# A parallel S4 + mixture-of-experts kernel: first operands, gates, squares and skip term in another order

## The chip, the cores and the metric

The kernel runs on one core of one Trainium2 chip. Its engines are TensorE (PE, matrix products), VectorE (DVE), ScalarE (ACT), GpSimd (POOL, here used only to issue DMAs that add in memory) and SyncE (SP, which issues the other DMAs). The metric is the device time of one execution in microseconds (us); less is better.

## What is computed

For `u` of 2048 tokens by D = 512 the output is a sum of three terms of the normalized rows:

```python
xn  = layernorm(x)                                   # x = u, over the 512 columns
y   = causal_convolution(xn, K) + xn * Dskip         # S4: K from A, B, C, log_dt; by FFT in the reference
moe = sum over e of gates[:, e] * (silu(xn @ w1[e]) @ w2[e])   # 8 experts, F = 1792
out = x + y + moe
```

The gates are the softmax of `xn @ w_gate` over all 8 experts (the top 8 of 8 are kept). All is float32. The two products of the experts are nearly all of the work on PE.

## The kernel before, in words

**Float32 by halves.** PE multiplies f16. Each operand is split into a high and a low f16 part, and each product is three matmuls (high by high, high by low, low by high). ACT writes a high part, DVE the low one (`hilo`, L432 and L435, for weights; L1181 and L1184 in `activate` for activations). So that the parts don't overflow, each weight matrix of each expert is scaled by a power of two that comes from the sum of its squares: ACT squares the weights as they are loaded (`square`, L429; tiles `pp`), DVE sums the rows (tile `r`, L390), PE sums over the partitions (`tot`, L166), ACT copies the sum out (`st`, L164), and a few short DVE steps make the power of two (`prepass_end`). A split of an expert's weight can't begin before its scale.

**Order of the work.** The loops run over expert e (8), token block tb (4 of 512 tokens) and d (4 groups of weight columns: `DQS`, pairs (0,1), (2,3), (4,5), (6)); each d has four slots s. A place is written (e, tb, d, s). `block()` forms the first product by seven Strassen products (`product`, L1162) in three PSUM tiles `hb`, with partial sums kept by ACT (`scC`, `sE`, `scB`, L1333) and added by DMAs from POOL. `pop(n)` issues second products `y` (L1146 to L1148), `flush` the low parts of the activations. The very first block (0, 0) is `plain()`: 14 products f = 0..13 of 12 matmuls each (L1384), without Strassen sums, in 16 slots of which 14 are used; its list of numbers says how many second products each slot issues, and after each product the activation is issued.

**Lists of side work.** `side`, `early` and `mid` map a place to functions that are issued there; `at(n, f)` counts slots from the start of the program (slot n is tb = n // 16 of expert 0). `slot()` (L1273) issues them, then `work_on(limit)`: the next one or two steps of the queue `work`, made by `plan(e)` for the next expert: squares (`piece_square`), the scale (`piece_end`), the splits of `w1` (`piece_w1`; of each raw weight, and of combined weights `tw` that DVE forms first) and of `w2` (`piece_w2`). Then `bg_run` issues steps of the S4 term, nearly all DVE work, as long as an account (`clock`, in estimated us of PE and DVE time) leaves room: a share of PE's time (`SHARE`). The engines take their instructions in the order of issue; semaphores between them come from the tiles.

**First operands.** Before the first product, `xplain(j)` normalizes 128 tokens (DVE), splits them (ACT high, DVE low) and transposes both parts on PE; `xplain_out(j)` copies the result from PSUM, by ACT for even j and DVE for odd j. `first_square` and `first_split` do the squares and splits of expert 0's `w1`, `first_scales` the scale; `keep_busy` issues matmuls without a use.

**Later operands.** The operands of a Strassen block are sums of quarters of x: `x_stats` (mean and 1/std), `x_sums` (DVE, L237 to L243), `x_high` (ACT, L249), `x_low` (DVE, L255), `x_turn` (PE transposes, L267, then a copy from PSUM by ACT or DVE, L271, L273, L278). The transposes, the gates (`gates_mm`, L339 and L342; `gates_dve`, L348 ff.) and the sums of squares share one PSUM bank, tag `s4`; `take_bank` hands it on. The statistics of the next tokens (`norm_sums`, L196) are DVE work too.

**Out of PSUM, and the skip term.** When the last product of a group of 128 tokens is in, `evacuate` scales it by its gate on ACT (L1124) into a tile `ye`, and a DMA from POOL adds it to `oacc` (L1126). `x + xn * Dskip` comes in by `base` (load, L1101), `base_add` (three DVE steps, L1107 to L1109) and `base_send` (a DMA from POOL), for four tiles of 128 tokens per token block. `ye` and `base` share four buffers, tag `stg`. A block's four `ye` come early in the next token block, at (e, tb + 1, 1, 1).

Of the kernel before, what the change touches and what calls it, by code (L numbers as in the profile page):

```python
# [32 lines left out]
def s4_moe_kernel(  # L33
# [61 lines left out]

    uts = {}

    clock = {"slot": 0, "pe": 0.0, "pe0": 0.0, "dve": 0.0, "dve0": 0.0, "left": 0.0}
    bank = {"out": None, "at": -1}

    def take_bank(out=None):
# [144 lines left out]
    def x_high(g, a):  # L246
        hi = xs_["hi"] = sb.tile([P, 7, TH], F16, tag="ta", name=f"xh{g}_{a}", bufs=1)
        for src, n0, n in xs_["f"]:
            S.copy(hi[:, n0:n0 + n, :].rearrange("p o d -> p (o d)"), src.rearrange("p o d -> p (o d)"))  # L249

    def x_low(g, a):
        hi = xs_["hi"]
# [5 lines left out]
    def x_turn(g, a, q):  # L258

        hi, lo = xs_["hi"], xs_["lo"]  # L260
        xv = xop.rearrange("p o a k t -> p (o a k) t")
        n = min(8, 28 - 8 * q)
        take_bank()
        tp = ps_s.tile([P, 8, P], F16, tag="s4", name=f"tp{g}_{a}_{q}")
        for r in range(n):
            o, b, k = (8 * q + r) // 4, (8 * q + r) // 2 % 2, (8 * q + r) % 2
            T.transpose(tp[:, r, :], (hi, lo)[b][:, o, k * P:(k + 1) * P], ident)  # L267
        if g == 1:
            dst = xv[:, 8 * q:8 * q + n, a * P:(a + 1) * P]
            if q % 2:  # L270
                V.tensor_copy(dst, tp[:, :n, :])  # L271
            else:
                S.copy(dst, tp[:, :n, :])  # L273
            if a and q == 3:
                nc.sync.dma_start(xd[1], xop)
        else:
            xs = sb.tile([P, 8, P], F16, tag="hh", name=f"xs{g}_{a}_{q}", bufs=9)
            S.copy(xs[:, :n, :], tp[:, :n, :])  # L278
            bank["at"] = now()
            nc.sync.dma_start(xd[g].rearrange("p o a k t -> p (o a k) t")[:, 8 * q:8 * q + n, a * P:(a + 1) * P],  # L280
                              xs[:, :n, :])
# [3 lines left out]
    def xplain(j, rs8):  # L285

        xn = sb.tile([P, D], F32, tag="fa", name=f"xn{j}")
        V.tensor_scalar(xn, uts[0][j], mean[:, j:j + 1], rs8[:, j:j + 1], op0=ALU.subtract, op1=ALU.mult)
        hl = sb.tile([P, 2, KT, P], F16, tag=("ta", "tt")[j % 2], name=f"xhl{j}", bufs=1)
        hlf = hl.rearrange("p a k t -> p a (k t)")  # L290
        S.copy(hlf[:, 0, :], xn)
        V.tensor_tensor(hlf[:, 1, :], xn, hlf[:, 0, :], op=ALU.subtract)
        xp[j] = ps_y.tile([P, 2 * KT, P], F16, tag=f"y{j}", name=f"tp{j}")
        for a in range(2):
            for k in range(KT):
                T.transpose(xp[j][:, a * KT + k, :], hl[:, a, k, :], ident)
# [130 lines left out]
    def square(e, w, pr, raw):  # L427
        rf = raw.rearrange("p a c -> p (a c)")
        S.activation(rf, rf, AF.Square, accum_out=rows_of(e, w)[:, pr:pr + 1])  # L429

    def hilo(dst, raw, sc):
        S.activation(dst[:, 0], raw, AF.Copy, scale=sc)  # L432
# [366 lines left out]

    act_later = []  # L800

    def tt_(n):

        return n / 960 + 0.14
# [200 lines left out]
    xplain_out(3)  # L1005
    keep_busy(6, ident)
    sq(5, True)
    sq(6)
    low1()
# [110 lines left out]
    def evacuate(e, i, y):  # L1120
        g = gates_e[e][:, i:i + 1]
        if e < E - 1 or i < NT - TPB:
            t = sb.tile([P, D], F32, tag="stg", name=f"ye{e}_{i}", bufs=4)
            S.activation(t, y, AF.Copy, scale=g)  # L1124
            if e:
                nc.gpsimd.dma_start(oacc[i], t, accum_op=ALU.add)  # L1126
            else:
                nc.sync.dma_start(oacc[i], t)
# [37 lines left out]

    tail = []

    def activate(e, tb, d, src, fh, th, whole=False):


        prs = (0, 1) if whole else DQS[d]
        n = len(prs)
        sc = scales[e]
# [6 lines left out]
        S.activation(ahl[:, 0, :n], fa, AF.Copy, scale=sc[:, 3:4])  # L1181

        def low():
            V.scalar_tensor_tensor(ahl[:, 1, :n], fa, sc[:, 3:4], ahl[:, 0, :n], op0=ALU.mult, op1=ALU.subtract)  # L1184
            clock["dve"] += tt_(n * TH)
            for q, pr in enumerate(prs):
# [24 lines left out]
        lows.append((first_split(2), True, False))  # L1211
    early, mid = {}, {}

    def at(n, f, where=side):
# [26 lines left out]
    for tb in range(NB):  # L1241
        for j in range(TPB):
            i = tb * TPB + j
            eb = (1, tb) if tb < NB - 1 else (2, 0)
            put((*eb, 1 + j // 2, j % 2), lambda i=i: base(i))
            put((*eb, 1 + j // 2, 2 + j % 2), lambda i=i: base_add(i))
            put((*eb, 1 + (j + 1) // 2, (3, 1)[j % 2]), lambda i=i: base_send(i))
        put((0, tb, 2, 0), lambda tb=tb: gates_mm(tb))
        put((0, tb, 2, 1), lambda tb=tb: gates_dve(tb))
# [6 lines left out]
    for n, (g, a) in enumerate(halves):  # L1256
# [13 lines left out]
    def slot(e, tb, d, s, pops):  # L1270
# [8 lines left out]
        for f in side.get((e, tb, d, s), ()):  # L1279
            f()  # L1280
        work_lows()
        work_on(2 if tb == NB - 1 or tb == 0 or e == 0 else 1)
        if (e, tb, d, s) >= (0, 2, 3, 1):
            if (e, tb, d, s) == (0, 2, 3, 1):
                clock["pe"] = clock["pe0"] = clock["dve"] = clock["dve0"] = 0.0
            bg_run()
        clock["slot"] += 1

# [19 lines left out]
    def block(e, tb, d):  # L1308
# [22 lines left out]
        def keep(tag, src):  # L1331
            t = sb.tile([P, 2, TH], F32, tag="sE" if tag == "sE" else "sCB", name=f"{tag}{e}_{tb}_{d}", bufs=1 if tag == "sE" else 3)
            S.copy(t[:, :n], src[:, :n])  # L1333
            return t
        begin(0)
        prod(A, 0, 0, True)
        S.copy(B[:, :n], A[:, :n])  # L1337
        if later:
            later.pop(0)()
        slot(e, tb, d, 0, pops[0])  # L1340
# [32 lines left out]
    def plain():  # L1373

        for f in range(NF):
# [90 lines left out]
```

## Time and profile before

| | us |
|---|---|
| median of 3 runs | 2415.65 |
| lowest, highest | 2413.35, 2416.8 |
| the profiled execution's own time | 2415.3 |
| its span, first to last instruction | 2413.5 |
| PE busy | 2354.6 |
| DVE busy | 1955.1 |
| ACT busy | 1426.2 |
| POOL busy | 339.2 |

A row of a timeline gives the start and the duration of an instruction (or of several alike, x12), its engine, line, operation, and out<-in; a bracket gives the idle time of the engine ahead of it and what ended it. In a list of waits a row gives total, number and longest. The granted clock is a share of TensorE's full speed; its mean over the span was 0.993.

### The profile page before, as it was taken

The page shows a single profiled execution, that of the slowest core. Times are in us where ns is not written, and L with a number is a line of the kernel's source. Part 1 is how long each engine was busy: PE and PEld are TensorE (multiplying, and loading weights), DVE is VectorE, ACT ScalarE, POOL GpSimd, SP SyncE. Part 2 cuts the span into 40 slices and gives each one's busy share as a digit, 9 for nine tenths or more (in the row PEclk, how much of TensorE's full clock was granted, in tenths as well). Part 3 has the DMA queues.
Part 4 walks back from the last instruction along what each step waited for, and adds up shares of the span by engine and source line. Part 5 has one row for each costly group of instructions (what it writes and reads, how often), then busy time and mean ns, then how long its engine had stood idle before and what let it go on. Part 6 is the DMA issues. An engine that isn't in the chain of part 4 may idle for free.

```text
span 2413.5 us, 44927 instructions
## 1 busy us (share of the span) xinstructions
PE 2354.6 (98%) x17663; PEld 1564.7 (65%) x17663; DVE 1955.1 (81%) x3836; ACT 1426.2 (59%) x2435; POOL 339.2 (14%) x394
## 2 busy tenths in 40 slices
PE   7789999999999999999999999999999999999999
PEld 4466666666666666666666666666666666666665
DVE  7663588689985999998889799999898799999611
ACT  6477575555646657565675566665575655754443
POOL 0000001211121110111110111111111101111112
PEclk9899999999999999999999999999999999999999
DMA  6466366574664645565465554655555644633356
GB/s 223 144 164 192 74 173 150 132 176 86 175 144 112 133 98 163 108 135 117 106 162 118 120 132 99 160 116 123 122 115 140 143 110 105 165 65 72 76 115 149
DMA packets 264644, 314.41 MB, mean 130 GB/s; under 512 B 124464, under 2 KB 158768, under 8 KB 264112
## 3 DMA queue, kind: packets, MB, share of 16 engines
q1 hardware_dynamic: 208560, 217.93, 29.6%
q0 software_dynamic: 55872, 93.61, 24.5%
q8 instruction: 138, 2.26, 0.4%
q14 instruction: 74, 0.61, 0.1%
HBM read 201.09 MB, written 60.82 MB: 109 GB/s over the span
## 4 chain that ended last, share of the span: by engine, by line
PE 82%; issue 7%; ACT 4%; DVE 3%; DMA 1%; POOL 1%; SPq 0%; DVEq 0%; POOLq 0%; ACTq 0%
PE hb L1162 36%; PE y L1146 14%; PE y L1148 14%; PE y L1147 14%; PE kgen L690 1%; ACT w1s L432 1%; PE yp L791 1%; PE kf L742 1%; PE uf L731 1%; PE hb L1384 1%; PE tp L267 1%; DVE w1s L435 1%; ACT fa L1179 0%; DMA oacc<-ye 0%; ACT ahl L1181 0%
## 5 line engine op out<-in xcount | busy, mean ns | idle before, releaser
L1162 PE MATMUL hb<-xop,w1s 128*128 128x256 f16 x9114 | 1074.9, 273 | 9.1 <-ACT scC L1333 6.8
L1162 PEld LDWEIGHTS <-w1s 128*128 128x128 f16 x9114 | 889.9, 98 | 186.9 <-issue 11.7
L1146 PE MATMUL y<-w2s,ahl 128*128 128x512 f16 x1792 | 680.6, 380 | 10.2 <-ACT ye L1124 10.2
L1148 PE MATMUL y<-w2s,ahl 128*128 128x512 f16 x1792 | 680.9, 380 | 0.0
L1147 PE MATMUL y<-w2s,ahl 128*128 128x512 f16 x1792 | 680.8, 380 | 0.0
L1148 PEld LDWEIGHTS <-ahl 128*128 128x128 f16 x1792 | 175.4, 98 | 212.1 <-issue 0.8
L1306 POOL DMA_DIRECT2D scC<-sE x124 | 111.6, 900 | 1363.6 <-ACT sE L1333 880.2
L1147 PEld LDWEIGHTS <-ahl 128*128 128x128 f16 x1792 | 175.4, 98 | 177.4 <-issue 12.3
L1146 PEld LDWEIGHTS <-ahl 128*128 128x128 f16 x1792 | 175.4, 98 | 165.2 <-issue 0.8
L774 DVE TENSOR_TENSOR s<-s,tm 128x720 f32<-128x720 f32 (+14 forms) x480 | 269.0, 560 | 16.6
L773 DVE TENSOR_TENSOR tm<-v,k 128x720 f32<-128x720 f32 (+14 forms) x480 | 267.7, 558 | 10.9
L1184 DVE SCALAR_TENSOR_TENSOR ahl<-fa,sc,ahl 128x512 f16<-128x512 f32 (+1 forms) x262 | 178.8, 683 | 90.1 <-ACT ahl L1181 90.0
L1179 ACT ACTIVATE fa<-hb,sc 128x512 f32<-128x512 f32 (+1 forms) x252 | 160.0, 635 | 149.7 <-PE hb L1162 141.1
L1344 ACT COPY hb<-hb 128x512 f32<-128x512 f32 x124 | 64.1, 517 | 261.6 <-PE hb L1162 261.6
L1181 ACT ACTIVATE ahl<-fa,sc 128x512 f16<-128x512 f32 (+1 forms) x262 | 175.9, 671 | 8.6
L1306 POOL DMA_DIRECT2D scB<-sE x124 | 107.2, 864 | 421.5 <-ACT scB L1333 291.1
L1184 DVE SCALAR_TENSOR_TENSOR ahl<-scB,sc,ahl 128x512 f16<-128x512 f32 x124 | 84.4, 681 | 100.0 <-ACT ahl L1181 98.6
L1337 ACT COPY hb<-hb 128x512 f32<-128x512 f32 x124 | 64.4, 519 | 167.1 <-PE hb L1162 165.6
L678 DVE TENSOR_TENSOR tb<-ta,tt 128x64 f32<-128x64 f32 (+2 forms) x192 | 132.2, 689 | 6.6
L676 DVE TENSOR_TENSOR ta<-tb,zr 128x64 f32<-128x64 f32 (+2 forms) x192 | 131.3, 684 | 3.4
L1126 POOL DMA_DIRECT2D oacc<-ye x108 | 96.1, 1308 | 259.9 <-ACT ye L1124 257.2
L677 DVE TENSOR_TENSOR tt<-tb,zi 128x64 f32<-128x64 f32 (+2 forms) x192 | 130.5, 680 | 0.0
(256 smaller groups left out, 2399.1 us busy)
## 6 DMA issues: line engine op xcount, KB each, us to landing
xop<-xd SPq DMA_DIRECT2D x210, 256.0 KB, 3.7
pp<-in_w_dram SPq DMA_DIRECT2D x98, 512.0 KB, 4.4
raw<-in_w_dram SPq DMA_DIRECT2D x56, 512.0 KB, 5.1
oacc<-ye POOLq DMA_DIRECT2D x108, 256.0 KB, 6.5
scC<-sE POOLq DMA_DIRECT2D x93, 256.0 KB, 4.2
scB<-sE POOLq DMA_DIRECT2D x93, 256.0 KB, 4.2
raw<-in_w_dram SPq DMA_DIRECT2D x52, 256.0 KB, 4.0
raw<-in_w_dram SPq DMA_DIRECT2D x104, 128.0 KB, 4.1
```

Source lines behind the costliest of these rows:

```text
L676: V.tensor_tensor(ta, tin, zrv, op=ALU.mult)
L678: V.tensor_tensor(tout, ta, tt, op=ALU.add)
L773: V.tensor_tensor(tm, v3f[:, :, 0:n], kb, op=ALU.mult)
L774: V.tensor_tensor(s3[:, :, m:], s3[:, :, m:], tm, op=ALU.add)
L1146: T.matmul(y, lhs[0], w2s[pr][:, 0, fh, :], start=(c == 0), stop=False)
L1147: T.matmul(y, lhs[0], w2s[pr][:, 1, fh, :], start=False, stop=False)
L1148: T.matmul(y, lhs[1], w2s[pr][:, 0, fh, :], start=False, stop=(c == NF - 1))
L1162: T.matmul(dst[:, q, :], w1s[pr][:, a, wo, k * P:(k + 1) * P], xop[:, xo, b, k, :], start=(first_mm and q == 0 and n == 0), stop=(n == 5), ...
L1179: S.activation(fa, src[:, :n], AF.Silu, scale=w1_unscale(e, d if whole else prs[0]))
L1181: S.activation(ahl[:, 0, :n], fa, AF.Copy, scale=sc[:, 3:4])
L1184: V.scalar_tensor_tensor(ahl[:, 1, :n], fa, sc[:, 3:4], ahl[:, 0, :n], op0=ALU.mult, op1=ALU.subtract)
L1306: nc.gpsimd.dma_start(dst, src, accum_op=ALU.add)
```

## The change

1. **First operands.** `xplain` is cut in two: the second half (`xplain_turn`: low part and transposes) is issued later. All four token groups come before the third square of `w1`; only j = 2 is copied out by DVE.
2. **First block.** The activation of f = 0 is issued behind product f = 1; the splits of `w1`, the squares and the scale of `w2` move by a slot or so; `norm_sums(1)` moves ahead of the sum of the `w2` squares (slot 5); the list of second products has fewer early and more late; `gates_split` goes to slot 12 and the gates of the first block to slots 16 and 17, which lie in (0, 1).
3. **Squares.** `clock["act"]` counts ACT's estimated time. Outside (0, 0) and the last token block of an expert, `work_on` gets a step only if the account has over 1.0 us of room (2 steps if 2.2 in expert 0). Before it was 2 steps in token blocks 0 and 3 and in expert 0, otherwise 1.
4. **Sums of squares** (`piece_end`) keep out of the slot before one in which `x_turn` comes (`turns`).
5. **Skip term.** Token blocks go to (1,1), (1,2), (2,1), (2,2) instead of (1,0), (1,1), (1,2), (2,0); both loads of a pair are issued in slot 0 of d = 1 (and d = 2), the sums in slots 1 and 2, both sends in slot 3.
6. `SHARE` is 1.0 instead of 0.96.

```diff
...
     def xplain(j, rs8):
-        hlf = hl.rearrange("p a k t -> p a (k t)")
-        S.copy(hlf[:, 0, :], xn)
-        V.tensor_tensor(hlf[:, 1, :], xn, hlf[:, 0, :], op=ALU.subtract)
+        S.copy(hl[:, 0].rearrange("p k t -> p (k t)"), xn)
+        xp[j] = (xn, hl)
+
+    def xplain_turn(j):
+
+        xn, hl = xp[j]
+        V.tensor_tensor(hl[:, 1].rearrange("p k t -> p (k t)"), xn, hl[:, 0].rearrange("p k t -> p (k t)"), op=ALU.subtract)
...
-        if j % 2:
+        if j == 2:
             V.tensor_copy(dst, xp[j])
...
         def later():
-            return now() > st["at"] + 1 and bank_free()
+            return now() > st["at"] + 1 and bank_free() and now() + 1 not in turns
...
+    def at_(n):
+
+        return n / 1050 + 0.17
...
     sq(0)
     sq(1)
     xplain(0, rs8_0)
+    xplain(1, rs8_0)
+    xplain_turn(0)
     V.tensor_reduce(row2[:, 0:1], rows_of(0, 0)[:, 0:2], axis=AX.X, op=ALU.add)
-    keep_busy(8, ident)
+    sq(2)
     stA = pow2_total(row2[:, 0:1], 1, "a")
     take_bank()
-    xplain(1, rs8_0)
+    xplain_turn(1)
+    keep_busy(8, ident)
+    xplain(2, rs8_0)
...
-    sq(2)
     xplain_out(0)
+    xplain_turn(2)
     low0 = first_split(0)
+    xplain(3, rs8_0)
     keep_busy(8, ident)
-    xplain(2, rs8_0)
+    xplain_out(1)
+    xplain_turn(3)
+    xplain_out(2)
     low0()
+    xplain_out(3)
+    keep_busy(8, ident)
     sq(3)
-    xplain_out(1)
-    keep_busy(8, ident)
-    xplain(3, rs8_0)
     sq(4)
-    xplain_out(2)
     low1 = first_split(1)
-    xplain_out(3)
-    keep_busy(6, ident)
...
-    SHARE = 0.96
+    SHARE = 1.0
...
+    def act_room():
+
+        clock["actleft"] = min(clock["actleft"], 2.0) + clock["pe"] - clock["pe1"] - clock["act"] + clock["act0"]
+        clock["pe1"], clock["act0"] = clock["pe"], clock["act"]
+        return clock["actleft"]
...
     for n in range(7):
-        at(n // 2, lambda n=n: first_square(1, n, second[n], n % 2 == 1))
-    at(0, first_scales, mid)
-    at(0, third)
+        at((n + 1) // 2, lambda n=n: first_square(1, n, second[n], n % 2 == 1))
+    at(1, first_scales, mid)
+    at(1, third)
     for n in range(4):
-        at(2 * n + 1, lambda n=n: plain_split(3 + n))
-    at(4, lambda: next(end_w2))
-    at(5, lambda: next(end_w2), mid)
-    at(6, lambda: fin(end_w2))
-    at(6, lambda: done.add("w2 scale"))
-    at(6, gates_split)
-    at(4, lambda: norm_sums(1))
+        at((2, 4, 5, 7)[n], lambda n=n: plain_split(3 + n))
+    at(5, lambda: norm_sums(1))
+    at(5, lambda: next(end_w2))
+    at(6, lambda: next(end_w2), mid)
+    at(7, lambda: fin(end_w2))
+    at(7, lambda: done.add("w2 scale"))
     at(7, lambda: x_stats(1))
+    at(12, gates_split)
+    at(16, lambda: gates_mm(0))
+    at(17, lambda: gates_dve(0))
...
-            eb = (1, tb) if tb < NB - 1 else (2, 0)
-            put((*eb, 1 + j // 2, j % 2), lambda i=i: base(i))
-            put((*eb, 1 + j // 2, 2 + j % 2), lambda i=i: base_add(i))
-            put((*eb, 1 + (j + 1) // 2, (3, 1)[j % 2]), lambda i=i: base_send(i))
+            eb = (1 + tb // 2, 1 + tb % 2)
+            put((*eb, 1 + j // 2, 0), lambda i=i: base(i))
+            put((*eb, 1 + j // 2, 1 + j % 2), lambda i=i: base_add(i))
+            put((*eb, 1 + j // 2, 3), lambda i=i: base_send(i))
...
         for q in range(4):
             at(s0 + 3 + q // 2, lambda g=g, a=a, q=q: x_turn(g, a, q), mid if q % 2 else early)
+            turns.add(s0 + 3 + q // 2 - 2)
...
-        work_on(2 if tb == NB - 1 or tb == 0 or e == 0 else 1)
+        room = act_room()
+        if e + tb == 0 or tb == NB - 1:
+            work_on(2)
+        elif room > 1.0:
+            work_on(1 if room < 2.2 or e else 2)
...
     def plain():
...
-            slot(0, 0, f // 4, f % 4, (0, 0, 0, 0, 0, 0, 0, 0, 2, 2, 3, 3, 3, 3)[f])
-            activate(0, 0, pr, hb[f % 3], fh, 0, True)
+            slot(0, 0, f // 4, f % 4, (0, 0, 0, 0, 0, 0, 0, 0, 0, 2, 2, 4, 4, 4)[f])
+            if f == 0:
+                continue
+            high = []
+            if f == 1:
+                activate(0, 0, 0, hb[0], 0, 0, True, high)
+            activate(0, 0, pr, hb[f % 3], fh, 0, True, high)
+            for g in high:
+                g()
```

(`activate` takes a list `wait` into which the step that writes the high part is put; `clock["act"]` is raised wherever ACT gets work.)

More of the change, by code (lines that the diff above doesn't have):

```diff
@@ L96, in s4_moe_kernel @@
     uts = {}
-    clock = {"slot": 0, "pe": 0.0, "pe0": 0.0, "dve": 0.0, "dve0": 0.0, "left": 0.0}
+    clock = {"slot": 0, "pe": 0.0, "pe0": 0.0, "dve": 0.0, "dve0": 0.0, "left": 0.0,
+             "act": 0.0, "act0": 0.0, "pe1": 0.0, "actleft": 0.0}
     bank = {"out": None, "at": -1}
@@ L249, in x_high @@
             S.copy(hi[:, n0:n0 + n, :].rearrange("p o d -> p (o d)"), src.rearrange("p o d -> p (o d)"))
+            clock["act"] += at_(n * TH)
     def x_low(g, a):
@@ L278, in x_turn @@
             S.copy(xs[:, :n, :], tp[:, :n, :])
+            clock["act"] += at_(n * P)
             bank["at"] = now()
@@ L429, in square @@
         S.activation(rf, rf, AF.Square, accum_out=rows_of(e, w)[:, pr:pr + 1])
+        clock["act"] += at_(D) + 0.7
     def hilo(dst, raw, sc):
@@ L1124, in evacuate @@
             S.activation(t, y, AF.Copy, scale=g)
+            clock["act"] += at_(D)
             if e:
@@ L1167, in s4_moe_kernel, with activate @@
     tail = []
-    def activate(e, tb, d, src, fh, th, whole=False):
+    def activate(e, tb, d, src, fh, th, whole=False, wait=None):
         prs = (0, 1) if whole else DQS[d]
         n = len(prs)
-        sc = scales[e]
         if fh == 0 or whole:
@@ L1180, in activate, with high @@
         ahl = sb.tile([P, 2, 2, TH], F16, tag="hh", name=f"ahl{e}_{tb}_{d}_{fh}{th}", bufs=9)
-        S.activation(ahl[:, 0, :n], fa, AF.Copy, scale=sc[:, 3:4])
+        def high():
+            S.activation(ahl[:, 0, :n], fa, AF.Copy, scale=scales[e][:, 3:4])
+        if wait is None:
+            high()
+        else:
+            wait.append(high)
+        clock["act"] += 2 * at_(n * TH)
         def low():
+            sc = scales[e]
             V.scalar_tensor_tensor(ahl[:, 1, :n], fa, sc[:, 3:4], ahl[:, 0, :n], op0=ALU.mult, op1=ALU.subtract)
@@ L1212, in s4_moe_kernel @@
     early, mid = {}, {}
+    turns = set()
     def at(n, f, where=side):
@@ L1243, in s4_moe_kernel @@
             i = tb * TPB + j
[L1244 to L1249 removed]
+            eb = (1 + tb // 2, 1 + tb % 2)
+            put((*eb, 1 + j // 2, 0), lambda i=i: base(i))
+            put((*eb, 1 + j // 2, 1 + j % 2), lambda i=i: base_add(i))
+            put((*eb, 1 + j // 2, 3), lambda i=i: base_send(i))
+        if tb:
+            put((0, tb, 2, 0), lambda tb=tb: gates_mm(tb))
+            put((0, tb, 2, 1), lambda tb=tb: gates_dve(tb))
     put((0, NB - 1, 2, 3), lambda: V.tensor_scalar(gates_e[1], gate[:, :, 1], scales[1][:, 4:5], None, op0=ALU.mult))
@@ L1281, in slot @@
         work_lows()
-        work_on(2 if tb == NB - 1 or tb == 0 or e == 0 else 1)
+        room = act_room()
[3 more added lines that the diff above has]
+            work_on(1 if room < 2.2 or e else 2)
         if (e, tb, d, s) >= (0, 2, 3, 1):
             if (e, tb, d, s) == (0, 2, 3, 1):
-                clock["pe"] = clock["pe0"] = clock["dve"] = clock["dve0"] = 0.0
+                clock["pe"] = clock["pe0"] = clock["pe1"] = clock["dve"] = clock["dve0"] = 0.0
             bg_run()
@@ L1333, in keep @@
             S.copy(t[:, :n], src[:, :n])
+            clock["act"] += at_(n * TH)
             return t
@@ L1337, in block @@
         S.copy(B[:, :n], A[:, :n])
+        clock["act"] += 2 * at_(n * TH)
         if later:
```

## Prediction

> **What bounds the kernel now.** I read the page first, then what TensorE (PE) waited for, then tables by stage around those waits, then the instructions of each place.
>
> ```profile
> span 2413.5 us, 44927 instructions
> ## 1 busy us (share of the span) xinstructions
> PE 2354.6 (98%) x17663; PEld 1564.7 (65%) x17663; DVE 1955.1 (81%) x3836; ACT 1426.2 (59%) x2435; POOL 339.2 (14%) x394
> ```
>
> PE is busy 98% of the span, and the change removes no product. So it can move only the 59 us in which PE isn't busy, and the clock after each. PE's waits, with their total, number and longest:
>
> ```profile
> PE tp L267 <- DVE lgs L348: 12.1, 1, 12.1
> PE tp L296 <- ACT xhl L291: 10.3, 4, 6.6
> PE y L1146 <- ACT ye L1124: 10.2, 4, 3.5
> PE hb L1162 <- ACT scC L1333: 6.8, 8, 1.2
> PE tp L267 <- ACT xs L278: 4.6, 2, 3.5
> PE tp L267 <- ACT st_w L164: 3.8, 2, 3.0
> PE tot_w L166 <- DVE r L390: 2.9, 1, 2.9
> PE hb L1162 <- ACT hb L1337: 2.4, 2, 2.1
> ```
>
> Tables by stage (us; then busy PE, weight load, DVE, ACT, POOL; granted clock; DMA; GB/s):
>
> ```profile
> 44.30:58.00 13.70, 13.70 (x70) 5.91 (x71) 12.70 (x47) 9.58 (x14) 0.00 (x0) 0.79 0.16 46
> 64.00:75.70 11.70, 0.00 (x0) 0.10 (x1) 9.60 (x18) 7.60 (x9) 0.00 (x0) 0.63 0.33 101
> ...
> 141.00:150.00 9.00, 5.46 (x31) 2.60 (x29) 2.79 (x9) 5.73 (x10) 0.86 (x1) 0.81 1.03 315
> 221.00:232.00 11.00, 7.97 (x50) 5.68 (x48) 4.04 (x9) 6.37 (x12) 0.00 (x0) 0.69 0.35 120
> 447.00:457.00 10.00, 6.48 (x33) 3.57 (x31) 2.23 (x4) 5.70 (x12) 4.01 (x5) 0.83 0.93 170
> ```
>
> In 64.00:75.70 PE does nothing and DVE has 9.60 of 11.7 us: here DVE sets the end. Where the clock column is below 1, a wait is paid again: at 0.83 over 10 us a product runs at half speed for 3.4 us, which costs 1.7 us.
>
> The profiled execution took 2415.3 us (1.8 us beside its span), 0.35 below the median; the sum is made against it. I did not carry the 0.35 over.
>
> **Part A: the front and the first block.**
>
> ```profile
> 24.03 3.80 PE L1384 MATMUL hb<-tb,w1s 128*128 128x512 f16 x12
> ...
> 51.35 0.14 DVE L185 TENSOR_SCALAR it_g<-kb_b 128x1 int32<-128x1 f32 x1
> ...
> 52.68 2.48 DVE L435 SCALAR_TENSOR_TENSOR w2s<-raw,sc,w2s 128x1024 f16<-128x1024 f32 x2
> ...
> 57.27 0.38 PE L1148 MATMUL y<-w2s,ahl 128*128 128x512 f16 x1
> 57.48 0.25 PE L339 MATMUL lg<-wgs,tb 128*128 128x16 f16 x4
> ...
> 58.29 0.59 PE L1384 MATMUL hb<-tb,w1s 128*128 128x512 f16 x2
> ...
> 67.68 1.28 DVE L435 SCALAR_TENSOR_TENSOR w1s<-tw,sA,w1s 128x1024 f16<-128x1024 f32 x1 [1.95 <-ACT w1s L432]
> 68.88 1.28 DVE L435 SCALAR_TENSOR_TENSOR w2s<-raw,sc,w2s 128x1024 f16<-128x1024 f32 x1
> 70.08 0.75 DVE L1184 SCALAR_TENSOR_TENSOR ahl<-fa,sc,ahl 128x512 f16<-128x512 f32 x1
> ...
> 71.88 0.95 DVE L255 TENSOR_TENSOR xl<-xfb,xh 128x768 f16<-128x768 f32 x1
> ...
> 75.74 0.37 PE L267 MATMUL tp<-ident,xh 128*128 128x128 f16 x2 [12.11 <-DVE lgs L348]
> ...
> 107.00 1.47 PE L1162 MATMUL hb<-xop,w1s 128*128 128x256 f16 x12
> ```
>
> Chaining the rows of the front in the new order (no square between the four copies, xplain's first halves early) I get the first product at some 19.3 instead of 24.03. That alone isn't a gain: PE then meets new waits (a product for the activation that is put off by one, a product for the split of the first combined weight, and tot_w, whose sum r now stands behind the four norm steps on DVE: longer than the 2.9 us of before). What decides is when the first transposed operand of the second x block is ready, because PE stands there 12.1 us.
>
> In before the turn waits twice over: for x_low (ends 72.83) and for the one PSUM bank, held until lgs. In after the gates of the first block come behind the first Strassen product, so only x_low is left. Ahead of x_low the order of after lacks on DVE: the low half of one combined w1 weight (68.88 - 67.68 = 1.2) and of one w2 weight (70.08 - 68.88 = 1.2), one low of an activation (0.75 at 70.08, of which 0.66 until the next may start), gates_split (52.68 - 51.35 = 1.33), and the 1.95 us in which DVE waits for ACT: 6.3 us. So x_low ends at 72.8 - 6.3 = 66.5. That it also starts earlier, I set against the new waits. From the first turn to the first Strassen product lay 107.00 - 75.74 = 31.3 us; after has 12 second products more in that stretch (they were done earlier before). A second product takes 57.48 - 57.27 = 0.21 us until the next matmul: 2.5 us. First Strassen product: 66.5 + 31.3 + 2.5 = 100.3, 6.7 earlier; the gates' small products, which in before stand ahead of the wait, come behind it and cost 58.29 - 57.48 = 0.8. **A = -5.9.** Bounds: 0, if the lowered DVE work only waits elsewhere; -10, if no new wait is worse than the old.
>
> **Part B: transposes and squares in the second to fourth block of expert 0.**
>
> ```profile
> 141.75 1.07 ACT L429 ACTIVATE pp<-pp 128x1024 f32<-128x1024 f32 x1
> 142.78 1.07 ACT L429 ACTIVATE pp<-pp 128x1024 f32<-128x1024 f32 x1
> ...
> 143.82 1.02 ACT L278 COPY xs<-tp 128x1024 f16<-128x1024 f16 x1
> ...
> 144.89 0.27 PE L267 MATMUL tp<-ident,xh 128*128 128x128 f16 x2 [3.54 <-ACT xs L278]
> ```
>
> Two squares of 1.03 us (142.78 - 141.75) stand on ACT ahead of the copy that frees the bank, and PE waits 3.54 us. The others here are st_w (3.8 in all), the second wait for xs (4.6 - 3.5 = 1.1) and hb L1337 (2.1 of its 2.4): 10.5, and 0.3 of the waits for scC: 10.8. With them go the half clocks of 141:150 (9.0 x 0.19 = 1.7) and of 221:232 (11 x 0.31 = 3.4, of which I take 3.0, since part of that stretch was idle): 15.5 us. The account lets a square through only when ACT has room, and piece_end keeps out of slots beside a turn, so st_w and the squares no longer stand in the turn's way. I keep 3.4 us: one bank wait behind four ye (1.3), one slot with two squares left (1.05), the rest 1. **B = -12.1**; bounds -15.5 and -9.
>
> **Part C: what the thinned squares put off.** The squares of expert 1 finish later, so its scale comes in block (0,2) instead of (0,1), and its first weight split in d=2 of (0,3) instead of d=0. Counting PE's work between the place where a weight's low half is issued and its first use, before has 30 us or more for each of expert 1; after has 0.7 us for the fifth w1 weight, 1.6 for its combination, 4.1 for a w2 weight, 3.5 and 0.1 for the sixth w1 weight and its combination.
>
> ```profile
> 338.26 0.27 PE L1355 MATMUL hb<-xop,ident 128*128 128x256 f16 x1
> ...
> 342.76 1.01 DVE L435 SCALAR_TENSOR_TENSOR w1s<-raw,sc,w1s 128x768 f16<-128x768 f32 x1
> ```
>
> This low half was issued beside the product at 338.26 and ended at 343.77: DVE was 5.5 us behind PE here, the worst; elsewhere between 240 and 375 us it was 2 to 3 us behind. At 2.5 us the first place costs 1.8, the second 0.9, which the first already pays in part, the last 2.4, part paid again. **C = +3.5.** Bounds: 0, if DVE is ahead, and the rival below.
>
> **Part D: the skip term.** ye and base share four buffers.
>
> ```profile
> 445.41 1.82 ACT L1124 ACTIVATE ye<-y,gse 128x512 f32<-128x512 f32 x3
> ...
> 446.38 2.91 POOL L1126 DMA_DIRECT2D oacc<-ye  x3 [8.93 <-ACT ye L1124]
> ...
> 447.29 0.38 PE L1146 MATMUL y<-w2s,ahl 128*128 128x512 f16 x1
> ...
> 450.88 0.69 ACT L1124 ACTIVATE ye<-y,gse 128x512 f32<-128x512 f32 x1 [3.64 <-DMA oacc<-ye]
> ...
> 451.62 0.38 PE L1146 MATMUL y<-w2s,ahl 128*128 128x512 f16 x1 [3.52 <-ACT ye L1124]
> ```
>
> Before, one base holds a buffer when a block's four ye come: three go at once, the fourth waits 3.64 us until the first ye's DMA lands, and PE waits 3.52 for the PSUM bank that the fourth would free. After, both bases of a pair are loaded in slot 0 and both hold buffers there: now the third ye waits for that same landing. PE needs the third's bank at 447.29 and would get it at some 451.5: 4.2 us. This comes in four blocks, (1,1), (1,2), (2,1), (2,2), where before it came in three and, at 0.9, in one (10.2 in all). By the other three landings I take 3.3, 3.7 and 3.7: 15.0 us. Half clocks: before one (447:457, 1.7), after three, 5.1. **D = 20.1 - 11.9 = +8.2.** Behind the waiting ye on ACT stand the fourth ye, which by then has its buffer, and the copies of the next Strassen sums; PE meets those only after the y products that wait too, so the time counts once. Bounds: +12, if all four waits are as long as a late landing; -2, if DMAs land sooner (their issue is on POOL, which is idle 8.93 us before).
>
> By the rows a wait of 2.9 us was followed by a clock of 0.79 and one of 3.54 by 0.81; I take three of the four new ones as followed so. The Trainium skill, "TensorE: Matmul & The Clock Gate", Part 1, says that the clock falls to half after an idle window of about 3.4 us. By it the first alone of the two rows would not have paid, and the sum would stay where it is; its later section "Why this matters for your kernels" draws the line at about 3 us, by which the fourth would pay too (rival 4).
>
> **Share of the S4 work and the rest: 0.** The background on DVE ends sooner, and the list of PE's waits has no row on a tile of S4. What it costs if DVE has no room left is in rival 3.
>
> Sum: -5.9 - 12.1 + 3.5 + 8.2 = -6.3, and 2415.3 - 6.3 = **2409**.
>
> **The rivals.**
>
> 1. *The first block's gain is lost.* x_low comes no earlier, since another DVE step or a transfer of x ends last there: A = 0, 2415. For it: DVE was busy 9.60 of 11.7 us, so any work added ahead of x_low (norm_sums(1) stands a slot later) counts in full. Against it: 12.1 us of wait hang on lgs, which is gone from there.
> 2. *The third ye doesn't wait.* If the first ye's DMA lands before PE needs the bank, or the next y products fill the time, D = -2: 2409 - 10.2 = 2399. Against it: the DMA took 4.5 us at 446.38.
> 3. *Slower: late weights in the first block of expert 1.*
>
> ```profile
> L774 DVE TENSOR_TENSOR s<-s,tm 128x720 f32<-128x720 f32 (+14 forms) x480 | 269.0, 560 | 16.6
> ```
>
> If DVE is 5.5 us behind at each place, as at 342.76, PE waits 5.5 - 0.7 = 4.8, 5.5 - 4.1 = 1.4 and 5.5 - 0.1 = 5.4: 11.6; two of them halve the clock (3.4); and with the larger share one more background step of 0.56 us stands ahead of each (1.7): 16.7 instead of 3.5, **2422**. It decides from the point where DVE stays over 5 us behind through d=2 and d=3 of (1,0). For it: DVE is busy 81% over the span and gets more work here. Against it: 5.5 was the worst of the places that I looked at.
> 4. *All four skip waits halve the clock*, the shortest too, as the 2.9 us one did: 1.7 more, 2411.
> 5. *The account doesn't clear the turns*: squares and st_w still stand before the copies, B = 0: 2421.
>
> **How the numbers follow.** Forecast 35% (its own range 2403 to 2414), rival 1 15%, rival 2 17%, rival 3 20%, rival 4 8%, rival 5 5%. A measurement of this kernel can tell about 0.2%, 4.8 us, from no change: faster is below 2410.8, slower above 2420.5. Faster: 25 of the forecast's 35, rival 2, half of rival 4: 46%. Slower: 18 of rival 3 and rival 5: 23%. Between: 31%. The range takes in rivals 2 and 3 with 1 or 2 us beside them: 2397 to 2423.
>
> **What would show it.** A right: first product near 19.3, tot_w waiting over 4 us, no wait on lgs, a turn waiting about 7 us until 66 to 67, first Strassen product near 100. B right: no wait over 1.5 us on xs or st_w between 130 and 232 us, clock 1.00 there. C right: a few waits of hb on DVE w1s between 370 and 440 us, together 3 to 4. D right: four waits of y on ye of 3.3 to 4.2 us. Wrong would be: another wait of PE over 3 us in a place not named here, or those of hb on w1s above 10 us.

## The result: slower by 0.5%, and the profile after

| | us |
|---|---|
| before, median of 5 runs beside it (2412.33 to 2416.8) | 2415.07 |
| after, median of 5 runs (2424.82 to 2430.79) | 2426.9 |
| ratio, 95% interval | 1.0052, 1.0038 to 1.0067 |
| after, the profiled execution and its span | 2430.79, 2429.0 |

The change makes the kernel 11.8 us slower; 2409 was forecast, and the time lies above the range. The profiled execution of after is 3.9 us above its median, so its span is 15.5 us longer than that of before. The page of after, and what PE waited for in it (total, number, longest):

```profile
span 2429.0 us, 44971 instructions
## 1 busy us (share of the span) xinstructions
PE 2360.4 (97%) x17657; PEld 1564.0 (64%) x17657; DVE 1955.7 (81%) x3835; ACT 1427.5 (59%) x2436; POOL 339.6 (14%) x394
```

```profile
PE y L1168 <- ACT ye L1145: 19.2, 7, 4.2
PE tp L303 <- ACT xhl L293: 7.5, 2, 7.2
PE hb L1425 <- ACT fa L1200: 6.4, 2, 5.3
PE hb L1184 <- ACT scC L1372: 5.9, 7, 1.0
PE hb L1184 <- ACT hb L1377: 5.1, 3, 1.8
PE tp L269 <- DVE xl L257: 4.9, 1, 4.9
PE tp L269 <- ACT xs L280: 3.9, 5, 1.1
PE hb L1184 <- ACT hb L1385: 3.6, 1, 3.6
PE tot_w L167 <- DVE r L397: 2.6, 1, 2.6
PE tp L269 <- ACT xh L250: 1.6, 1, 1.6
PE hb L985 <- POOL ident masks.py:199: 1.4, 1, 1.4
PE hb L1184 <- DVE w1s L443: 0.9, 1, 0.9
```

The wait on lgs (12.1 us) and those on st_w are gone, as forecast. The wait on ye has nearly doubled, and one of hb on ACT L1385 (L1344 in before) is new. Where the time goes shows best in the start of the same matmul in both timelines:

| first product of | before | after | after - before |
|---|---|---|---|
| (0,0) | 24.03 | 19.41 | -4.6 |
| (0,1), d = 0 | 107.00 | 102.13 | -4.9 |
| (0,1), d = 1 | 126.8 | 129.3 | +2.6 |
| (0,2), d = 2 | 239.9 | 230.7 | -9.2 |
| (1,1), d = 0 | 415.3 | 407.3 | -8.0 |
| (2,3), d = 0 | 861.1 | 873.6 | +12.5 |
| end of the span | 2413.5 | 2429.0 | +15.5 |

By stage in after (us; busy PE, weight load, DVE, ACT, POOL; granted clock; DMA; GB/s):

```profile
58.00:70.00 12.00, 5.49 (x28) 2.58 (x27) 11.48 (x20) 7.71 (x10) 0.00 (x0) 0.85 0.53 167
100.00:120.00 20.00, 16.38 (x132) 10.22 (x131) 13.05 (x49) 4.59 (x8) 0.00 (x0) 0.94 0.59 209
136.00:150.00 14.00, 13.06 (x106) 9.00 (x104) 7.62 (x14) 12.76 (x20) 1.05 (x2) 1.00 0.61 176
215.00:232.00 17.00, 16.06 (x127) 10.97 (x125) 6.68 (x12) 13.39 (x20) 1.72 (x2) 1.00 0.56 147
436.00:446.00 10.00, 6.05 (x33) 3.42 (x32) 3.26 (x5) 5.23 (x11) 4.41 (x5) 0.80 0.54 75
446.00:456.00 10.00, 10.00 (x59) 6.04 (x58) 8.87 (x25) 5.42 (x10) 2.85 (x4) 0.86 0.78 150
```

The third and fourth rows answer to 141:150 and 221:232 of before: PE is nearly always busy there, at full clock. The last two show what a wait on ye costs: 4 us idle, and then a clock of 0.86 although PE is busy all the time (the record has it at 0.50 from 441.97 to 448.80). The new wait at 115 us, by queue (SP, then ACT, then PE):

```profile
104.35 0.33 SPq L277 DMA_DIRECT2D xd<-xop  x1
108.53 2.76 SPq L127 DMA_DIRECT2D ut<-in_u_dram  x4
111.33 0.91 SPq L427 DMA_DIRECT2D pp<-in_w_dram  x2
```

```profile
103.64 0.57 ACT L1377 COPY hb<-hb 128x512 f32<-128x512 f32 x1 [0.30 <-PE hb L1184]
116.95 1.06 ACT L436 ACTIVATE pp<-pp 128x1024 f32<-128x1024 f32 x1 [12.74 <-DVE ib L209]
117.92 0.19 ACT L436 ACTIVATION_READ_ACCUMULATOR pp<-pp 128x1 f32 x1
118.01 0.58 ACT L1385 COPY hb<-hb 128x512 f32<-128x512 f32 x1
```

```profile
118.64 1.23 PE L1184 MATMUL hb<-xop,w1s 128*128 128x256 f16 x5 [3.62 <-ACT hb L1385]
```

The load of the third x block (`ut`) goes into the tile that holds the first block's operands, which the gates now read until 108.5. It waits on SP, and behind it stands the load of a weight to be squared (`pp`, 111.33). ACT stands 12.74 us in front of that square, and behind the square stands the copy that PE needs. (The bracket names DVE L209, which has no part in `pp`; the load is what the square reads. It landed at 116.70, and the square began at 116.95.)

### The profile page after: what moved, and what is told of

Same layout as the page of the kernel before. It is cut to its first block, busy times and chain, and to the rows that moved or that the text cites. A ratio compares the mean times of both kernels' runs of the same rounds, so it can differ in the third digit from the quotient of the medians.

```text
span 2429.0 us, 44971 instructions
## 1 busy us (share of the span) xinstructions
PE 2360.4 (97%) x17657; PEld 1564.0 (64%) x17657; DVE 1955.7 (81%) x3835; ACT 1427.5 (59%) x2436; POOL 339.6 (14%) x394
## 4 chain that ended last, share of the span: by engine, by line
PE 77%; issue 11%; DVE 5%; ACT 3%; DMA 3%; POOL 1%; SPq 0%; DVEq 0%; POOLq 0%; ACTq 0%
PE hb L1184 33%; PE y L1168 13%; PE y L1169 13%; PE y L1170 13%; PE kgen L698 1%; PE kf L750 1%; PE yp L799 1%; DMA oacc<-ye 1%; DVE ahl L1213 1%; DVE w1s L443 1%; PE uf L739 1%; ACT w1s L440 1%; POOL scB L1345 1%; PE hb L1425 1%; PE tp L269 0%
## 5 line engine op out<-in xcount | busy, mean ns | idle before, releaser
L1184 PE MATMUL hb<-xop,w1s 128*128 128x256 f16 x9114 | 1074.5, 273 | 15.5 <-ACT scC L1372 5.9
L1168 PE MATMUL y<-w2s,ahl 128*128 128x512 f16 x1792 | 682.7, 381 | 19.2 <-ACT ye L1145 19.2
L781 DVE TENSOR_TENSOR tm<-v,k 128x720 f32<-128x720 f32 (+14 forms) x480 | 267.8, 558 | 11.1
L1385 ACT COPY hb<-hb 128x512 f32<-128x512 f32 x124 | 64.1, 517 | 247.5 <-PE hb L1184 247.5
L1204 ACT ACTIVATE ahl<-fa,sc 128x512 f16<-128x512 f32 (+1 forms) x262 | 175.7, 671 | 11.8 <-PE y L1170 2.4
L1213 DVE SCALAR_TENSOR_TENSOR ahl<-scB,sc,ahl 128x512 f16<-128x512 f32 x124 | 84.3, 680 | 100.3 <-ACT ahl L1204 100.3
L1377 ACT COPY hb<-hb 128x512 f32<-128x512 f32 x124 | 64.5, 520 | 162.8 <-PE hb L1184 161.7
L1213 DVE SCALAR_TENSOR_TENSOR ahl<-scC,sc,ahl 128x512 f16<-128x512 f32 x124 | 84.3, 680 | 69.0 <-ACT ahl L1204 64.6
```

The lines of the kernel that those rows point to most:

```text
L781: V.tensor_tensor(tm, v3f[:, :, 0:n], kb, op=ALU.mult)
L1168: T.matmul(y, lhs[0], w2s[pr][:, 0, fh, :], start=(c == 0), stop=False)
L1184: T.matmul(dst[:, q, :], w1s[pr][:, a, wo, k * P:(k + 1) * P], xop[:, xo, b, k, :], start=(first_mm and q == 0 and n == 0), stop=(n == 5), ...
L1204: S.activation(ahl[:, 0, :n], fa, AF.Copy, scale=scales[e][:, 3:4])
```

## The experiments

Each took 4 to 12 runs beside 9 to 21 of the kernel before on the same chip, whose median was 2414.6 to 2415.4 in every group. "After" is 2426.9.

### The skip term and the shared buffers

The rows of after in (2,1), on ACT:

```profile
743.06 1.25 ACT L1145 ACTIVATE ye<-y,gse 128x512 f32<-128x512 f32 x2
748.29 0.69 ACT L1145 ACTIVATE ye<-y,gse 128x512 f32<-128x512 f32 x1 [3.98 <-DMA oacc<-ye]
750.53 0.69 ACT L1145 ACTIVATE ye<-y,gse 128x512 f32<-128x512 f32 x1 [1.55 <-DMA oacc<-ye]
```

Two ye go at once, the third waits for the first's landing, and the fourth waits again, for the second's. Two kernels tell the buffers from ACT's new timing.

**b_skip_new**: the kernel before with the new slots alone.

```diff
-            eb = (1, tb) if tb < NB - 1 else (2, 0)
-            put((*eb, 1 + j // 2, j % 2), lambda i=i: base(i))
...
+            eb = (1 + tb // 2, 1 + tb % 2)
+            put((*eb, 1 + j // 2, 0), lambda i=i: base(i))
...
```

> The kernel before with the skip term's new slots alone. Theory (buffers: both bases of a pair hold two of the four buffers when the four ye come, so the third ye waits for the landing of the first ye's addition, and each such wait is followed by a half clock): four waits of y on ACT ye of 3.5 to 4.3 us in (1,1), (1,2), (2,1), (2,2), and +15 to +20 us, 2430 to 2435. Rival (the waits in the changed kernel come from ACT, whose squares are dealt out differently there): the waits stay as in the kernel before, at most 5 us more, 2415 to 2420.

Measured: 2446.94, ratio 1.0132 (1.0118 to 1.0146), 32 us slower.

```profile
PE y L1146 <- ACT ye L1124: 17.8, 8, 4.1
PE yp L791 <- DVE z L781: 13.9, 1, 13.9
```

The waits on ye come with the slots, not with ACT's account (those of the third ye were 4.1, 2.9, 4.0 and 2.9 us, two of them shorter than expected). But 32 is more than 20: a wait of 13.9 us for the S4 work (`z`, which DVE makes for the S4 products `yp` on PE) is new as well, ahead of (7,3), where the kernel issues whatever is left of it.

**a_skip_late**: after, with the skip term one d later.

```diff
-            put((*eb, 1 + j // 2, 0), lambda i=i: base(i))
-            put((*eb, 1 + j // 2, 1 + j % 2), lambda i=i: base_add(i))
-            put((*eb, 1 + j // 2, 3), lambda i=i: base_send(i))
+            put((*eb, 2 + j // 2, 0), lambda i=i: base(i))
+            put((*eb, 2 + j // 2, 1 + j % 2), lambda i=i: base_add(i))
+            put((*eb, 2 + j // 2, 3), lambda i=i: base_send(i))
```

> The changed kernel with loads, sums and sends of the skip term one d later (d = 2 and 3 instead of 1 and 2), so that no base holds a buffer when the four ye come; token blocks and slots within d are kept. Theory (buffers): no wait of y on ACT ye is left, the 19 us of waits and the 8 to 10 us of half clock behind them go: 24 to 30 us less, 2397 to 2403. Rival (the additions themselves, or the loads, are what the transfers wait for): the waits turn up again at the new place, and the time stays above 2415.

Measured: 2396.14, 0.9922 (0.991 to 0.9935): 30.8 us below after. PE's waits between 430 and 860 us, of a_skip_late:

```profile
PE hb L1184 <- ACT scC L1372: 0.8, 1, 0.8
PE hb L1184 <- ACT hb L1377: 0.4, 1, 0.4
```

No wait on ye is left, and none has taken its place. From one token block's first product to the next, (1,1), (1,2), (2,1) and (2,2) take 69.5, 74.1, 73.8 and 71.3 us instead of 77.5, 80.3, 82.2 and 79.8: 31.1 us, of which 19.2 are the waits. About the end of each of the four waits after's clock falls to 0.50 for 6.83 us; half of the time that PE works in these stretches makes 11.1 us. The 0.7 that is left is mostly work of S4 on PE, which the two kernels have in different token blocks.

### The S4 work and its share

**a_share**: after with `SHARE = 0.96`.

> The changed kernel with the share of the S4 work as it was, 0.96. Theory (a fuller DVE comes late with the combined weights at the turn of an expert, ACT then stands in a weight's split while PE waits for the copy into hb): the three waits of hb on ACT L1377 at the first slot of (3,0), (4,0) and (6,0), 5.1 us in all, go: 2421 to 2424. Rival (the squares dealt out differently put ACT late there): these waits stay, 2425 to 2428.

Measured: 2453.72, 1.0157 (1.0143 to 1.0171), 27 us slower than after. Both theories had it faster or equal. The waits of hb on ACT L1377 did go, all of them, as the theory said, so they come with the larger share (those on scC grow by 3.2 us in their place); but the smaller share costs far more. PE's largest waits from 2300 us on (`kf` is another product of S4, whose operand `kt` a DMA brings):

```profile
PE yp L799 <- DVE z L789: 21.3, 2, 19.4
PE kf L750 <- DMA kt<-kd: 7.2, 1, 7.2
```

The larger share, which I had costed at nothing, is what keeps the S4 work from running into the end. **b_skip_late** and **b_oldtb_late**: the kernel before with the skip term at d = 2 and 3, in the new token blocks or in its own.

```diff
 # b_skip_late
+            eb = (1 + tb // 2, 1 + tb % 2)
 # b_oldtb_late
             eb = (1, tb) if tb < NB - 1 else (2, 0)
 # both
+            put((*eb, 2 + j // 2, 0), lambda i=i: base(i))
...
```

> The kernel before with the skip term in token blocks (1,1), (1,2), (2,1), (2,2), one d later (d = 2 and 3), nothing else changed. Theory (buffers): no wait of y on ACT ye; the 10.2 us of waits and 1.7 us of half clock behind them go: 2402 to 2405. Rival (the S4 work is issued later with these slots, as the profile of the kernel before with the new slots showed a wait of 13.9 us for it ahead of (7,3)): the waits on ye go, but PE waits 10 to 30 us ahead of (7,3): 2412 to 2435.

> The kernel before with the skip term one d later (d = 2 and 3), but in its own token blocks (1,0), (1,1), (1,2), (2,0). Theory (it is the new token blocks, with the sums of expert 1's first block moved to expert 2's, that put the S4 work one step behind at a share of 0.96): no wait for yp ahead of (7,3), no wait of y on ACT ye, 2401 to 2405. Rival (any shift of the skip term by a d does it): 13.9 us of wait for yp, 2416 to 2420.

Measured: b_skip_late 2418.89, 1.002 (1.0011 to 1.0029); b_oldtb_late 2403.23, 0.9955 (0.9942 to 0.9967). Of b_skip_late:

```profile
PE yp L791 <- DVE z L781: 13.9, 1, 13.9
```

and the largest of b_oldtb_late, which are those of before without the ones on ye:

```profile
PE tp L267 <- DVE lgs L348: 12.1, 1, 12.1
PE tp L296 <- ACT xhl L291: 11.0, 4, 7.3
PE hb L1162 <- ACT scC L1333: 6.6, 7, 1.8
```

So it is the token blocks. The 480 additions of S4 on DVE (`s<-s,tm`): how many were begun before the first product of a block, counted in the traces:

```
             before  b_oldtb_late  b_skip_late  b_skip_new  a_share  after
(2,2)            77            77           75          75       75     93
(3,0)           120           120          105         105      105    123
(7,2)           465           465          439         439      428    468
```

The gap opens in (2,2) and (2,3) and is not made up (in a_share it grows to 30 by (6,0)): with the new blocks, sums of the skip term stand in (2,1) and (2,2), and the account takes 2.0 us of DVE's time off for each. That a share of 0.96 then has no room to make it up is what these counts suggest; why the loss is just one group of 15 wasn't tried apart.

**a_late_load_96** has 0.96 in after with the skip term one d later and the load of the next section.

> The changed kernel with the skip term one d later, the load one slot later, and the share of before, 0.96. Theory (with the new token blocks 0.96 is too little whatever else is in place): waits of 14 to 30 us for yp ahead of (7,3), 2403 to 2420. Rival (the 29 us came from the waits on ye, which cost the account's slots): no such wait, 2386 to 2391.

Measured: 2424.08, 1.0038 (1.0026 to 1.0051), 31 us above the same kernel with 1.0, and 4 above the range expected.

```profile
PE yp L799 <- DVE z L789: 22.0, 2, 19.4
```

There is no wait on ye in it: the waits on the buffers have no part in the loss. **b_late_share**: b_skip_late with `SHARE = 1.0`.

> The kernel before with the skip term one d later in (1,1) to (2,2), and the share of the S4 work 1.0 instead of 0.96. Theory (with the new token blocks the S4 work needs the larger share to be done ahead of (7,3)): the 13.9 us of wait for yp go, and what the late skip term gains is left: 2402 to 2406. Rival (the S4 work is late for another reason, such as a step that waits for a slot): the wait stays, 2416 to 2420.

Measured: 2419.19, 1.0016 (1.0007 to 1.0025): a miss in time; the rival has the time right, but not the reason. The 13.9 us went, and these came from 900 us on (the profiled execution, 2424.29, is the longest of the twelve):

```profile
PE kf L742 <- DMA kt<-kd: 9.5, 2, 5.4
PE hb L1162 <- ACT hb L1337: 4.8, 3, 1.8
```

With squares dealt out as before, a share of 1.0 brings a transfer of S4 late in (3,2) and (5,2), and ACT late at an expert's turn; after has only the second. **a_late_load_98** takes 0.98.

> The changed kernel with the skip term one d later, the load one slot later, and a share of 0.98. Theory (the share has a threshold, below which the S4 work reaches into (7,3), and above it costs some 1.8 us at the turn of an expert): either the S4 work is done in time and the waits of hb on ACT L1377 go, 2387 to 2391, or it is late and PE waits some 14 us ahead of (7,3), 2403 to 2408. Rival (the share sets no wait at an expert's turn): 2391 to 2395.

Measured: 2389.3, 0.9888 (0.9873 to 0.9903), 3.6 us below the same with 1.0, though the intervals overlap. The largest waits from 900 to 2300 us:

```profile
PE hb L1184 <- ACT scC L1372: 4.0, 5, 0.8
PE hb L1184 <- ACT hb L1377: 3.6, 2, 1.8
```

In time at 0.98, late at 0.96: a threshold lies between. Of after's three waits of hb on L1377 (5.1 us) one is gone.

### The front and the first block

**a_load**: after, the load one slot later.

```diff
-    at(16, lambda: load_x(2))
-    at(17, lambda: x_stats(2))
+    at(17, lambda: load_x(2))
+    at(18, lambda: x_stats(2))
```

> The changed kernel with the load of the third x block one slot later (17 instead of 16; its statistics in 18). Theory (queue: this load waits on SP until the gates' products have read the old tile, and the load of the first square's weight stands behind it; ACT then waits 12.7 us in that square, and the copy into hb stands behind the square): no wait of hb on ACT at the first Strassen block's second slot, 3.6 us of wait and some 3 us of half clock less: 2419 to 2422. Rival (the weight's load waits for its own buffer, or for the transfer of the operands ahead of it): the square waits as long and the time stays at 2425 to 2428.

Measured: 2421.93, 1.0027 (1.0018 to 1.0036): 5.0 below after. Between 100 and 130 us PE has no wait at all (after: 3.6); the load behind the gates was the cause. **a_late_load** puts it together with the late skip term.

> The changed kernel with the skip term one d later and the load of the third x block one slot later. If the two causes are separate their gains add: 2396 - 5 = 2391 (2389 to 2394). If the load's place matters only while the clock is halved behind that wait by chance, less: 2394 to 2397.

Measured: 2392.86, 0.991 (0.9896 to 0.9923), 3.3 below a_skip_late: in the range for separate causes, though the intervals overlap. In the profile of a_skip_late the wait of 3.62 us for the load is still there, but no half clock follows it (last section), so in that execution the load's place could win the wait alone. On a_late_load stand four more.

**a_late_load_front** has the order of the first operands of before (the diff's hunks on `xplain` and the front undone).

> As the one with both, but with the first operands in the order of the kernel before. Theory (what decides the first block's end is DVE's work ahead of x_low, not the first product): first product 4.6 us later, but at most 2 us of it left at the first Strassen product; within 2 us of the one with both. Rival (the head start carries through): 4 to 6 us slower.

Measured: 2394.69, 0.9919 (0.9905 to 0.9932). The first product comes 5.5 us later (24.67), the first Strassen product 3.1 (103.52), the end 1.8: most of the head start is lost in waits.

**a_late_load_gates**: `gates_split` in slot 7, the gates of the first block in 8 and 9.

> As the one with both, but the gates of the first block in the first block (split in slot 7, products in 8, the rest in 9) as in the kernel before. Theory (the gates' DVE work and their hold of the PSUM bank stand ahead of the second block's transposes): a wait of tp on lgs is back, the first Strassen product comes 4 to 7 us later, 2396 to 2400. Rival (the gates' work fits beside x_low): within 2 us of the one with both, 2391 to 2395.

Measured: 2398.09, 0.9926 (0.9914 to 0.9938), 5.2 slower, with

```profile
PE tp L269 <- DVE lgs L355: 5.1, 1, 5.1
```

**a_late_load_tw**: `clock["slot"] > 2 * pr + 2` in `piece_sums`, instead of `+ 1`.

> As the one with both (late skip term, late load), but the combined weights of expert 0 may be begun one slot later. Theory (in the first block ACT stands 5 us in the split of a combined weight whose data aren't there, and the activation that frees PE's bank is behind it, but the first block's end is set by DVE's work ahead of x_low): the wait of 3.8 to 5.3 us near 37 us goes, and at most 1.5 us of it is left at the end: 2391 to 2394. Rival (PE's wait carries through): 2388 to 2390.

Measured: 2390.33, 0.9894 (0.9881 to 0.9907), 2.5 faster, between the two ranges, and the intervals overlap. From 30 to 70 us:

```profile
PE tot_w L167 <- DVE r L397: 7.1, 1, 7.1
PE tp L269 <- DVE xl L257: 4.9, 1, 4.9
PE tp L269 <- ACT xh L250: 1.3, 1, 1.3
```

The wait for the activation (3.8 us in a_late_load) is now one for r, 7.1 instead of 2.9, and the first Strassen product comes 1.6 us earlier (98.89): most of what PE no longer waits for at one place it waits for at the next, which suggests that DVE's chain is the bound here.

**a_late_load_acct**: squares by the old rule (`work_on(2 if tb == NB - 1 or tb == 0 or e == 0 else 1)`, without `turns`).

> As the one with both (skip term one d later, load one slot later), but squares dealt out as in the kernel before (2 steps or 1, no account, no turns). Theory (the account cleared the transposes' way, -11.8 us of waits and half clock in (0,1) and (0,2), paid back in part by three late copies into hb of 5.1 us): 6 to 12 us above the one with both, waits of tp on ACT xs and st_w back between 130 and 232 us. Rival (it is the order of the front that shifted the transposes away from the squares): within 3 us of the one with both.

Measured: 2415.03, 1.0003 (0.9994 to 1.0012), 22 us slower, well above the 6 to 12 expected (the profiled execution, 2410.71, is the shortest of the eleven). Between 100 and 260 us, where a_late_load has 3.9 us of waits on xs alone:

```profile
PE tp L269 <- ACT xs L280: 4.1, 2, 3.0
PE hb L1184 <- ACT hb L1373: 4.1, 2, 3.8
PE tp L269 <- ACT st_w L165: 3.8, 2, 3.0
```

and 7.5 us of kf on kt<-kd in (3,2) and (5,2), as in b_late_share. The account, with `turns`, is the best part of the change; its cost isn't the copies into hb, which are there under either rule.

**a_best** has the late skip term, the late load, the later combined weights and 0.98.

> The changed kernel with the skip term one d later, the load of the third x block and the combined weights of expert 0 one slot later, and a share of 0.98. If the gains add: 2393 - 3.5 (share) - 2.5 (combined weights) = 2387. If the two are one and the same wait of the front: 2389 to 2391.

Measured: 2387.59, 0.9892 (0.9876 to 0.9907): the lowest median, 27.6 us below the kernel before beside it (2415.2). But its ratio is no lower than that of a_late_load_98 (0.9888), so whether the combined weights add to the share isn't shown.

## Why the prediction was wrong, point by point

| step | forecast | profiled executions | |
|---|---|---|---|
| A: to the end of the first Strassen quarter | -5.9 | +2.6 | (0,1), d = 1 |
| B: transposes and squares | -12.1 | -11.8 | +2.6 to -9.2 |
| C: late weights | +3.5 | +1.2 | -9.2 to -8.0 |
| D: the skip term | +8.2 | +20.5 | -8.0 to +12.5 |
| share and rest | 0 | +3.0 | +12.5 to +15.5 |
| sum | -6.3 | +15.5 | |

By this table the forecast missed by 21.8 us, of which D makes 12.3, A 8.5 and the share 3.0; C came out 2.3 lower.

**A** failed at "the gates' small products, which in before stand ahead of the wait, come behind it and cost 0.8". Up to there it was near: first product at 19.41 (forecast 19.3), x_low ready for PE at 68.46 (66.5), first Strassen product at 102.13 (100.3). I had counted the gates' matmuls, not who waits for what they read: `load_x(2)` overwrites their operands and now stood ahead of weight loads on SP. That turned 0.8 into 7.5: 3.62 of wait, and 2.95 of clock behind it (5.90 us of work at a clock of 0.50, from 117.71 to 124.54); a_load gives 5.0 of it back. It was also the sign that the forecast had named: a wait over 3 us in a place not named there. Of the waits of the front, tot_w was smaller than I thought (2.6), and one of 5.3 us, ACT in the split of a combined weight, larger; both stand beside DVE's chain and, as far as a_late_load_tw shows, decide little. (Of the squares of `w1` it is the fourth, `sq(3)`, that comes behind all four token groups; the third stands between the first two groups and the last two.)

**B** was right in mechanism and size: before loses 10.5 us of waits and 4.7 of half clock in this stretch, after 3.7 of waits. So it was no luck; a_late_load_acct shows that the account does it, and more (22 us in all, since it also spares S4's transfers late in the program).

**C** was smaller: one wait of hb on w1s of 0.9 us. (The step of the table also holds the 0.9 us that before waits for ye in (1,0), which the forecast has under D.) The slower rival built on it didn't occur.

**D** was right in mechanism, wrong in size. The four waits of the third ye were 3.95, 3.92, 3.99 and 4.22 us by the timeline (16.1; forecast 15.0). Missed were the waits of the fourth ye in three of the blocks, 3.1 us; I had written that it "by then has its buffer", but its buffer is that of the second ye, and it waits for that one to land. And the clock: 11.1 us behind the waits instead of 5.1. All four were followed by a half clock (rival 4 had that), and each lost 2.8 us to it in the mean, where I had taken 1.7: the half clock lasted 6.83 us, not 3.4. By the Trainium skill, "TensorE: Matmul & The Clock Gate", Part 1, an idle window of about 3.4 us halves the clock. All four waits were longer than that, and so far the trace agrees; but a_skip_late has one of 3.62 us with the clock at 1.00 behind it, and the kernel after has one of 2.56 us with the clock at 0.50 behind it, so here the length of a wait doesn't decide (last section).

**Share: 0** was wrong in what it says. The trace of before showed that PE never waits for S4, and I took that as room. It was room of one kind: the last step of S4 on DVE ended at 2276.6 us, 47 us ahead of (7,3), and the new token blocks alone use that up (13.9 us of wait in b_skip_late). The larger share wins 27 us back (a_share): S4 ends at 2286, 54 us ahead of (7,3). The forecast put both at nothing. The three waits at the turns of experts, 5.1 us together, were not foreseen either; with 0.96 they are not there (a_share, a_late_load_96).

Rival 3, the slower one, was given 20% for the wrong mechanism; none of the rivals had the load, the fourth ye or S4 coming late at the end. The changed kernel with the skip term in its old token blocks wasn't tried.

## What to carry to other kernels

When a step that reads a tile is moved later, look for the load that overwrites this tile and for what stands behind that load in its queue. Price a wait of PE with the clock that follows it: here 19.2 us of waits cost 30. And an end that isn't waited for isn't free: measure how far ahead of its user it is, and what of it each moved step takes.

## What the runs showed of the hardware that I had not expected

What a wait of PE costs beside itself depends on where it falls, and not only on its length. In the profiles the granted clock is 1.00 or 0.50, and it changes only on a grid of 3.41 us, which begins at another offset in each execution. The same wait of 3.62 us, of hb on ACT L1385, in after (from 115.02 on) and in a_skip_late (from 114.39 on), by stretches of that grid (columns as before; the clock follows POOL):

```profile
114.29:117.71 3.42, 0.73 (x4) 0.22 (x3) 2.99 (x14) 0.76 (x1) 0.00 (x0) 1.00 0.68 270
117.71:124.54 6.83, 5.90 (x26) 3.78 (x26) 5.61 (x16) 5.34 (x11) 0.00 (x0) 0.50 0.41 138
```

```profile
112.79:116.20 3.41, 1.60 (x8) 0.61 (x7) 3.17 (x12) 0.00 (x0) 0.00 (x0) 1.00 0.73 282
116.20:119.62 3.42, 1.61 (x15) 1.45 (x15) 1.92 (x12) 3.26 (x6) 0.00 (x0) 1.00 0.34 86
119.62:126.45 6.83, 6.83 (x53) 4.98 (x52) 6.09 (x13) 5.47 (x10) 1.03 (x1) 1.00 0.60 182
```

In after 2.7 us of the wait lie in one stretch, and the clock is halved for the next two. In a_skip_late the grid cuts the wait in two, 1.8 us on each side, and the clock stays. Over the 17 profiles, from 30 us to the last product on PE, a stretch at full clock with up to 1.83 us idle was always followed by full clock, one with 2.14 us or more always by half; between these both occur. So for waits of 2.2 to 3.6 us, where the profiles have both outcomes, it is in part chance whether the clock falls behind them. The wait of 2.56 us for tot_w in after lay whole in one stretch, and 3.41 us at a clock of 0.50 followed.
